# A later load of v, its scaling one chunk on, and three places in the order of the seven-product steps

## The chip, the cores and the metric

The kernel runs on one core of one Trainium2 chip. The core has five engines with queues of their own: TensorE (PE in the profile; PEld is its loading of weights), VectorE (DVE), ScalarE (ACT), GpSimd (POOL) and SyncE (SP, which here only issues transfers). The time is that of one execution on the device, in microseconds; less is better. The figure to compare is the median of the runs.

## The reference: what is computed

A recurrent attention with decay (4 batches, 8 heads, 768 positions, 64 numbers per head) feeds a two-layer network with 3072 tokens, 512 inputs and 2048 hidden units. All is in 32-bit floats, but the two weight matrices come as 64-bit floats and are turned into 32-bit ones by the kernel.

```python
for t in range(S):
    state = gamma[None, :, None, None] * state + np.einsum('bhd,bhe->bhde', k[:, :, t], v[:, :, t])
    y[:, :, t] = scale * np.einsum('bhd,bhde->bhe', q[:, :, t], state)
x = y.transpose(0, 2, 1, 3).reshape(B * S, H * D)
h = x @ w_in
g = h - np.tanh(h)
out = g @ w_out
```

## The kernel before

**Attention in chunks.** The 3072 tokens are cut into 24 chunks of 128 (`ci`), six for each batch. q and v are multiplied by powers of the decay (`scale`, line 267), and k and q are needed transposed. The first eight chunks are worked in a piece order written by hand (lines 991 to 1012). From chunk 8 on the transposing is done by a DMA: ACT copies k and q into a tile `apart` (`set_apart`, line 314), ACT issues a transfer that writes it to a scratch tensor `rows` in HBM, and SP issues a transposing DMA from `rows` into `kqT` (`turn_by_dma`, line 321), which has to wait until `rows` has landed. PE then makes the chunk's products (`products`, line 339: first k with v at L350, then the transposed k and q at L356) and its outputs (`outputs`, `outputs_rest`, L405), and ACT copies the outputs into `xT` (`keep_x`, L451).

**The network in tiles.** A tile (n, m2) is 256 tokens by 256 hidden units. An "up" product makes h in PSUM, ACT and DVE make g of it (th, u, q0, q1, large; `shrink_...`), and "down" products of g with w_out are summed in PSUM. For n of 0 to 3 the products are ordinary: eight matmuls at L471 for an up, eight at L560 for a down. From n = 4 (`FAST_UP`, `FAST`) both are done with seven products in place of eight: the up in two groups, U (products 1, 5, 7, 6) and V (2, 3, 4) at L801. Between them `up_take` (L806) copies what U left in PSUM out on ACT, POOL adds pairs of it (`up_pairs`, L811), V overwrites a part of the same PSUM bank, so it waits for the copy, and `up_add` (L816, L818) adds the pairs on DVE. The down products of these tiles are at L700.

**What sets the order.** Every engine works in the order in which the program issues to it. The loop from line 1100 on runs over steps `s`, one tile each; `with_chunk` puts a chunk step (`chunk_step`, line 1072) into two of every three steps: in steps 9, 11, 12, 14, 15, 17, 18 and so on to 35 and 37. The chunk step of `ci` makes the products of chunk ci + 2, loads k, q and v of chunk ci + 4 (`load_chunk`, all on SP), and turns chunk ci + 3. The step before it scales q and v of chunk ci + 3 on POOL (lines 1109 to 1111), in front of the weight conversions of that step. SP's queue thus reads, chunk by chunk: k, q, v, the transposing DMA, then weight loads. k and q have two buffers each, v has four.

Step 32 (`FIRST_UP`) is the first with seven products up. In steps 32 and 34 `downs(lag, half)` still issues down products of the old kind (L560) for the last tiles before, four matmuls for each half of a tile; step 33 has none, since the distance between up and down grows by one there. `middle()` (line 1066) gives ACT the square q0 and DVE the multiplication by it.

For n = 6 and 7 a list of pieces, `tile_order` (line 1256), orders each tile: U, the copy c, the pairs P, ..., M, V, R, E, the addition a, .... M and E issue as many of the open down products as `MIDDLE` and `END` say for that tile; M stops at the end of a run of eight tiles, and R then reads the sums out.

Of the kernel before, what the change touches and what calls it, by code (L numbers as in the profile page):

```python
# [31 lines left out]
def kernel(  # L32
# [25 lines left out]
    nc = tc.nc  # L58
# [64 lines left out]
    def weight_ends(i):  # L123


        f, r = divmod(i, 2 * NC)
        if r < NC:
            cols = ts(NC * f + r, P)
            rows = w_in[:, cols].rearrange("(k two p) n -> p two k n", two=2, p=P)

            return w1[:, :, cols], [
                (ds(0, P), 0, rows[:, 0]),
                (ds(0, D), 1, rows[D:, 1]),
                (ds(D, D), 1, rows[:D, 1]),
            ]
        m = NC * f + r - NC
        return w2[:, m], w_out[ts(m, P)]

    def load_weights(i):
        if i >= NW:  # L140
            return
        dst, src = weight_ends(i)
        raw = None
        if w_out.dtype != F32:
            if EARLY <= i < EARLY + 2 * len(rooms):
                raw = rooms[(i - EARLY) // 2][:, (i - EARLY) % 2]
            else:
                raw = stage.tile([P, 2 * BANK], U32, tag="raw", name=f"raw_{i}", bufs=3)
            raws[i] = raw
        if not isinstance(src, list):  # L150
            if raw is None:
                nc.sync.dma_start(out=dst, in_=src)
            else:
                nc.sync.dma_start(out=raw, in_=src.bitcast(U32))
            return
        if raw is not None:
            dst = raw.rearrange("p (c n) -> p c n", c=NC)
        for r, k, w in src:
            nc.sync.dma_start(out=dst[r, k::2], in_=w if raw is None else w.bitcast(U32))
# [87 lines left out]
    def load_one(ci, which, queue=nc.sync):  # L247
        if ci >= NCH:
            return
        b, j = divmod(ci, CPB)  # L250
        nm, src = ("k", "q", "v")[which], (k, q, v)[which]
        t = inp.tile([P, H, D], F32, tag=nm, name=f"{nm}_{ci}", bufs=4 if nm == "v" else 2)
        rows = src[b, :, ts(j, P), :]
        if nm == "q" and ci < WIDE:
            queue.dma_start(
                out=t.rearrange("p (i r) d -> p i (r d)", r=RUN),
                in_=rows.rearrange("(g i) (p r) d -> p g i (r d)", i=2, r=RUN),
            )
        else:
            queue.dma_start(out=t, in_=rows.rearrange("h p d -> p h d"))  # L260
        loaded.setdefault(ci, {})[which] = t

    def load_chunk(ci):
        for which in range(3):
            load_one(ci, which)

    def scale(ci, which, engine):
        if ci >= NCH:
            return
        t, g = loaded[ci][1 + which], (gw if ci < WIDE else gq, gv)[which]  # L270
        out_ = t
        if which == 0 and ci < WIDE:
            if not wide:
                room = mid.tile([P, 2, RUN, 2, D], F32, tag="apart", name="wide", bufs=1)
                wide.extend([room[:, i % 2] for i in range(WIDE)])
            out_ = loaded[ci][1] = wide.pop()
            out_ = out_.rearrange("p r i d -> p i r d")
            t, g = (x.rearrange("p (i r) d -> p i r d", r=RUN) for x in (
                t, g[:, ts(ci % CPB, H)][:, :, None].to_broadcast([P, H, D])))
        else:  # L280
            g = g[:, ts(ci % CPB, H)][:, :, None].to_broadcast([P, H, D])
        engine.tensor_tensor(out_, t, g, op=ALU.mult)  # L282
# [205 lines left out]
    def shrink_factor(n, m2):  # L488
        q0 = work("q0", 1)
        nc.scalar.activation(q0, shrinking[n, m2]["u"], AF.Square, bias=bias0)  # L490
        shrinking[n, m2]["q0"] = q0
# [194 lines left out]
    def fast_down(n, m2, first, last, half=None):  # L686
        some = fast_order(first)[{None: slice(7), 0: slice(4), 1: slice(4, 7)}[half]]
        if first and 1 in some:
            fast_banks(n)
        fast_products(n, m2, first, last, some)  # L690
# [40 lines left out]
    def fast_end(n):  # L731


        todo, store = sums_of(n)
        for x in ("p1", "c11", "v"):
            todo[x]()
        for x in ("w", "c22", "x", "c21", "c12"):
            def step(x=x):
                todo[x]()
                if x[:2] == "c1" or x == "c21":  # L740
                    store(int(x == "c21"))
            ending.append(step)
# [62 lines left out]
    def up_take(n, m2):  # L805
        nc.scalar.copy(out=odd_room[0], in_=hps[n, m2])  # L806
# [53 lines left out]
    def part(j, n, m2, first, last):  # L860
        down(n, m2, j, first, last)
        if last:
            add_up(n, m2, j)

    def downs(lag, half=None):

        while len(waiting) > lag:
            tile_ = waiting[0] if half == 0 else waiting.pop(0)
            if tile_[0] >= FAST:
                fast_down(*tile_, half=half)  # L870
                if tile_[3] and half != 0:
                    fast_end(tile_[0])
            else:
                for j in range(2) if half is None else (half,):
                    part(j, *tile_)
            if half is not None:
                return
# [145 lines left out]
    FIRST = 8  # L1023
# [3 lines left out]
    with_chunk = {h // 2: FIRST - 3 + i for i, h in enumerate(halves)}  # L1027
# [5 lines left out]
    FIRST_UP = steps.index((FAST_UP, 0, True, False))  # L1033
# [30 lines left out]
    before = None  # L1064

    def middle():

        if before and len(shrinking[before]) == 2:
            shrink_factor(*before)
            shrink_third(*before)  # L1070
# [29 lines left out]
    for s in range(BEGUN, steps.index((PAIRED - 2, 0, True, False))):  # L1100
        n, m2, first, last = steps[s]
        fast = n >= FAST_UP
        ci = with_chunk.get(s)

        falls_back = s == FALL or s in behind_up
        lag = LAG + int(s >= FALL)
        if ci is not None and not falls_back:
            chunk_step(ci)
        if s + 1 in with_chunk:
            for which in range(2):  # L1110
                scale(with_chunk[s + 1] + 3, which, nc.gpsimd)
        for i in with_weights.get(s, []):
            convert(i)
        if fast:
            fast_up(n, m2, (1, 5, 7, 6))
            up_take(n, m2)
        else:
            for i in range(2):
                up(n, m2, i)
        if falls_back and ci is not None:  # L1120
            chunk_step(ci)
        if before and ci is not None:
            turn_and_see(ci)
        if ci == NCH - 2:
            outputs(ci + 1)
            see(ci + 1)
        for i in with_weights.get(s, []):
            load_weights(i + 3)
        waiting.append(steps[s])
        if fast:  # L1130
            if before and ci is None:
                shrink_factors(*before)
                shrink_last_factor(*before)
            up_pairs()
            for make in with_sums.get(s, []):
                make()
            downs(lag, 0)
            if not before:
                downs(lag, 1)
            fast_up(n, m2, (2, 3, 4))  # L1140
            up_add(n, m2)
            shrink_begin(n, m2)
            if before:
                shrink_end(*before)
                if before[0] >= FAST:
                    fast_sums(*before)
            downs(lag, 1)
            end_some(1)
            shrink_two(n, m2)
            before = n, m2  # L1150
            if s + 1 not in with_chunk:
                middle()
        else:
            shrink_begin(n, m2)
            shrink_factors(n, m2)
            shrink_multiply(n, m2)
            downs(lag)
            shrink_last_factor(n, m2)
            shrink_end(n, m2)
            for make in with_sums.get(s, []):  # L1160
                make()
# [72 lines left out]
    def ripe():  # L1234
# [13 lines left out]
        "M": lambda n, m2, *_: next_products(MIDDLE[PAIRS * (n - PAIRED + 2) + m2]),  # L1248
        "E": lambda n, m2, *_: next_products(END[PAIRS * (n - PAIRED + 2) + m2]),
        "R": lambda *_: end_run(),  # L1250
# [4 lines left out]
    }  # L1255
    tile_order = """U c P q1- f2- x M V R E a S l- thA uA f3- f4- f0A q0A R f1A s"""
    MIDDLE = (2, 4, 4, 4, 6, 3, 4, 5, 4, 5, 5, 5, 4, 6, 5, 5)
    END = (0, 1, 2, 3, 4, 0, 2, 4, 2, 0, 1, 3, 1, 0, 2, 1)
    for n in range(PAIRED - 2, PAIRED):
        for m2 in range(PAIRS):  # L1260
            waiting.append((n, m2, m2 == 0, m2 == PAIRS - 1))
# [2 lines left out]
            before = n, m2  # L1264
# [4 lines left out]
    for j in range((NB - FIRST_BLOCK) * PAIRS):  # L1269
# [7 lines left out]
        before = other  # L1277
# [71 lines left out]
```

## Time and profile before

| | us |
|---|---|
| median of 3 runs | 693.65 (693.26 to 694.98) |
| the profiled execution, its own time | 695.14 |
| its span | 693.4 |

The granted clock of TensorE was 1.00 through the whole span. The span holds three stretches: the attention and ordinary products to about 285 us, the seven-product steps to about 478 us, and seven-product blocks of two tiles to the end. The slices of the page (40 of 17.3 us each, in tenths) show where transfers are heavy:

```profile
POOL 1632454555355586877854464364343446454271
PEclk9999999999999999999999999999999999999999
DMA  8892267968788566500000000000000000000000
```

Nearly all transfers are over by 295 us. Queue q1 is that of SP, q10 that of ACT; q8 and q14 carry instructions. The loads of k, q and v are 256 KB each in rows of 256 B, the write of `rows` is 512 KB:

```profile
## 3 DMA queue, kind: packets, MB, share of 16 engines
q1 hardware_dynamic: 116736, 50.08, 28.2%
q10 hardware_dynamic: 2736, 8.83, 3.6%
q8 instruction: 48, 0.79, 0.5%
...
rows<-apart ACTq DMA_DIRECT2D x16, 512.0 KB, 4.8
k<-in_k_dram SPq DMA_DIRECT2D x24, 256.0 KB, 4.8
q<-in_q_dram SPq DMA_DIRECT2D x24, 256.0 KB, 4.9
v<-in_v_dram SPq DMA_DIRECT2D x24, 256.0 KB, 5.9
```

The last column is the median time from issue to landing. In the timelines, a row gives the start, the length, the engine, the line, what is written and read, the shape and the number of instructions merged; in brackets stand the idle time of the engine before it and what ended that.

### The profile page before, as it was taken

To read this page: it belongs to the slowest core of one execution; us is meant where nothing else is said; L and a number is where in the kernel's file an instruction comes from. 1 tells how busy PE (TensorE), PEld (TensorE's weight loads), DVE (VectorE), ACT (ScalarE), POOL (GpSimd) and SP (SyncE) were. 2 spreads that over 40 slices of the span, in tenths; PEclk is the share of its full clock that TensorE was granted. 3 is DMA by queue.
4 is the path that set the end of the run, shared out by engine and by line. 5 is a ranking of instruction groups with operands and counts; after the bars stand their busy time and mean duration, and the time that the engine had idled before them with its cause. 6 is when DMAs were issued, how large, how long until landed. Compare 5 with 4: busy or idle time off the path is not lost.

```text
span 693.4 us, 15454 instructions
## 1 busy us (share of the span) xinstructions
PE 684.4 (99%) x6092; PEld 557.5 (80%) x6092; DVE 531.0 (77%) x879; ACT 429.4 (62%) x817; POOL 356.7 (51%) x492
## 2 busy tenths in 40 slices
PE   8999999999999999999999999999999999999998
PEld 5776666667667667779999999999888888888886
DVE  4999999989798865677776787687878779668641
ACT  3787577776776855465555666566766666566520
POOL 1632454555355586877854464364343446454271
PEclk9999999999999999999999999999999999999999
DMA  8892267968788566500000000000000000000000
GB/s 223 228 279 67 85 170 205 233 163 218 209 191 222 160 167 180 157 33 1 1 1 16 17 1 31 1 1 30 2 1 31 1 1 30 1 0 31 1 30 31
DMA packets 119544, 59.89 MB, mean 86 GB/s; under 512 B 101680, under 2 KB 112560, under 8 KB 119472
## 3 DMA queue, kind: packets, MB, share of 16 engines
q1 hardware_dynamic: 116736, 50.08, 28.2%
q10 hardware_dynamic: 2736, 8.83, 3.6%
q8 instruction: 48, 0.79, 0.5%
q14 instruction: 24, 0.20, 0.1%
HBM read 35.83 MB, written 14.68 MB: 73 GB/s over the span
## 4 chain that ended last, share of the span: by engine, by line
PE 88%; DMA 6%; ACT 3%; DVE 2%; SPq 1%; issue 0%; ACTq 0%; DVEq 0%
PE h L801 14%; PE o L560 13%; PE h L471 13%; PE fast_t L700 12%; PE y L700 8%; PE fast_o L840 7%; PE h L840 7%; PE fast_o L700 6%; PE y L405 3%; DMA kqT<-rows 3%; DMA rows<-apart 3%; PE last_h L700 1%; PE s L356 1%; PE s L350 1%; ACT apart L318 1%; PE kqTp L298 1%
## 5 line engine op out<-in xcount | busy, mean ns | idle before, releaser
L471 PE MATMUL h<-xT,w 128*128 128x256 f32 x512 | 117.7, 382 | 0.0
L560 PE MATMUL o<-w,g 128*128 128x512 f32 x256 | 116.3, 596 | 0.0
L471 PEld LDWEIGHTS h<-xT,w 128*128 128x128 f32 x512 | 95.9, 190 | 21.5 <-issue 9.1
L560 PEld LDWEIGHTS o<-w,g 128*128 128x128 f32 x256 | 47.6, 190 | 46.7 <-issue 44.0
L850 POOL TENSOR_TENSOR fast_head<-fast_head 128x512 f32<-128x512 f32 x16 | 20.5, 1278 | 87.2 <-ACT fast_head L846 87.2
L490 ACT ACTIVATE q<-u,tab 128x512 f32<-128x512 f32 x88 | 63.6, 723 | 1.4
L509 DVE TENSOR_TENSOR th<-h,th 128x512 f32<-128x512 f32 x72 | 49.1, 682 | 19.3 <-ACT th L482 17.2
L208 POOL TENSOR_TENSOR low<-low,power 128x512 f32<-128x512 f32 x26 | 34.5, 1326 | 52.6 <-DVE power L201 40.3
L1166 ACT ACTIVATE th<-h 128x512 f32<-128x512 f32 x32 | 19.1, 597 | 51.5 <-DVE h L818 30.3
L513 DVE SCALAR_TENSOR_TENSOR h<-q,h 128x512 f32<-128x512 f32 x72 | 49.8, 692 | 1.0 <-ACT q L490 1.0
L217 POOL TENSOR_TENSOR w<-low,head 128x512 f32<-128x512 f32 x28 | 36.9, 1317 | 13.5 <-DVE low L208 6.4
L282 POOL TENSOR_TENSOR q<-q,tab 128x512 f32<-128x512 f32 x16 | 18.0, 1125 | 46.6 <-DMA q<-in_q_dram 46.6
L801 PEld LDWEIGHTS h<-xT,w 128*128 128x128 f32 x256 | 37.4, 191 | 5.5 <-ACT fast_head L806 2.3
L811 POOL TENSOR_TENSOR fast_head<-fast_head 128x256 f32<-128x256 f32 x32 | 23.4, 731 | 35.5 <-ACT fast_head L806 35.5
L801 PE MATMUL h<-xT,w 128*128 128x128 f32 x256 | 39.8, 278 | 0.5 <-ACT fast_head L806 0.5
L552 DVE COPY_PREDICATED g<-large,th 128x512 f32<-128x512 int32 x39 | 35.8, 918 | 3.9
L816 DVE TENSOR_TENSOR h<-h,fast_head 128x256 f32<-128x256 f32 x32 | 13.8, 431 | 31.2 <-PE h L801 26.2
L650 POOL TENSOR_TENSOR s<-g 128x128 f32<-128x128 f32 x38 | 18.9, 497 | 36.5 <-DVE g L552 29.6
L522 DVE SCALAR_TENSOR_TENSOR g<-q,h 128x512 f32<-128x512 f32 x32 | 22.0, 687 | 17.3 <-ACT q L1174 9.8
L1174 ACT ACTIVATE q<-u,tab 128x512 f32<-128x512 f32 x49 | 35.2, 719 | 0.0
L1179 ACT ACTIVATE large<-u,tab 128x512 f32<-128x512 f32 x49 | 35.0, 715 | 0.0
L484 ACT ACTIVATE th<-h 128x512 f32<-128x512 f32 x16 | 9.6, 598 | 40.3 <-DVE h L818 40.3
(298 smaller groups left out, 1874.1 us busy)
## 6 DMA issues: line engine op xcount, KB each, us to landing
rows<-apart ACTq DMA_DIRECT2D x16, 512.0 KB, 4.8
k<-in_k_dram SPq DMA_DIRECT2D x24, 256.0 KB, 4.8
q<-in_q_dram SPq DMA_DIRECT2D x24, 256.0 KB, 4.9
v<-in_v_dram SPq DMA_DIRECT2D x24, 256.0 KB, 5.9
raw<-in_moe_w_out_dram SPq DMA_DIRECT2D x12, 512.0 KB, 4.3
out_dram<-sum SPq DMA_DIRECT2D x22, 256.0 KB, 2.2
raw<-in_moe_w_in_dram SPq DMA_DIRECT2D x14, 256.0 KB, 4.0
raw<-in_moe_w_in_dram SPq DMA_DIRECT2D x28, 128.0 KB, 4.1
```

The lines of the kernel that those rows point to most:

```text
L217: engine.tensor_tensor(dst, low, head, op=ALU.add)
L471: nc.tensor.matmul(hp, w1[:, c, ts(2 * m2 + i, P)], xT[n // 2][:, c, ts(n % 2, TH)], start=(begins and c == 0), stop=(c == NC - 1), skip_g ...
L490: nc.scalar.activation(q0, shrinking[n, m2]["u"], AF.Square, bias=bias0)
L509: nc.vector.tensor_tensor(th, hp, th, op=ALU.subtract)
L513: nc.vector.scalar_tensor_tensor(hp, in0=shrinking[n, m2]["q0"], scalar=C0, in1=hp, op0=ALU.add, op1=ALU.mult)
L552: nc.vector.copy_predicated(flat, large.bitcast(I32), th)
L560: nc.tensor.matmul(o_p[n, j], gT[n, m2][:, i, ts(j, P)], w2[:, 2 * m2 + i], start=(first and i == 0), stop=(last and i == 1))
L700: nc.tensor.matmul(accs[n][k], left[k - 1], right, start=first and k in (1, 6, 7, 4), stop=last, skip_group_check=True)
L801: nc.tensor.matmul(hps[n, m2][:, ts(PLACE[k], P)], s_of[m2][k - 1][:, c], x_of[n][k - 1][:, c], start=(k == 1 and c == 0), stop=(c == 1), ...
L840: nc.tensor.matmul(hps[2 * b + i, m2][:, ts(place, TH)], s_of[m2][k - 1][:, c], x_of["block", b][k - 1][:, c], start=(k in (1, 5) and c == 0),
L1174: nc.scalar.activation(q1, shrinking[n, m2]["u"], AF.Square, bias=bias1, scale=math.sqrt(A))
L1179: nc.scalar.activation(large, shrinking[n, m2]["u"], AF.Relu, bias=bias_m)
```

## The change

There are five edits. The load of v leaves `load_chunk` and comes at the end of the step's issues, behind the transposing DMA and the step's weight loads. v of a chunk is scaled one chunk step later than before, so in the step just before the one that uses it; POOL still does q first. In step 32 the second half of an old down product is issued behind V rather than in front of it. `middle()` for the tile of step 33 is called behind the `up_take` of step 34 rather than at the end of step 33. Two numbers of `END` are smaller by one.

```diff
     def load_chunk(ci):
-        for which in range(3):
+        for which in range(2):
             load_one(ci, which)
...
         if s + 1 in with_chunk:
-            for which in range(2):
-                scale(with_chunk[s + 1] + 3, which, nc.gpsimd)
+            scale(with_chunk[s + 1] + 3, 0, nc.gpsimd)
+            if with_chunk[s + 1] + 2 >= FIRST:
+                scale(with_chunk[s + 1] + 2, 1, nc.gpsimd)
...
             fast_up(n, m2, (1, 5, 7, 6))
             up_take(n, m2)
+            if s == FIRST_UP + 2:
+                middle()
...
         for i in with_weights.get(s, []):
             load_weights(i + 3)
+        if ci is not None:
+            load_one(ci + 4, 2)
         waiting.append(steps[s])
...
             downs(lag, 0)
-            if not before:
-                downs(lag, 1)
             fast_up(n, m2, (2, 3, 4))
             up_add(n, m2)
             shrink_begin(n, m2)
...
             before = n, m2
-            if s + 1 not in with_chunk:
+            if s + 1 not in with_chunk and s != FIRST_UP + 1:
                 middle()
...
-    END = (0, 1, 2, 3, 4, 0, 2, 4, 2, 0, 1, 3, 1, 0, 2, 1)
+    END = (0, 1, 1, 2, 4, 0, 2, 4, 2, 0, 1, 3, 1, 0, 2, 1)
```

## The prediction

> **What bounds the kernel now.** I read the busy row first, then the list of waits for PE alone, then the timelines around each wait.
>
> ```profile
> PE 684.4 (99%) x6092; PEld 557.5 (80%) x6092; DVE 531.0 (77%) x879; ACT 429.4 (62%) x817; POOL 356.7 (51%) x492
> ...
> PE s L356 <- DMA kqT<-rows: 1.6, 3, 0.9
> ...
> PE y L405 <- ACT xT L451: 0.6, 1, 0.6
> PE h L801 <- ACT fast_head L806: 0.5, 2, 0.3
> ```
>
> PE is busy 99% of the span. The change removes no matmul, so it can only win back time in which PE stands still. The three lower rows are all of PE's waits between 100 and 420 us (us in total, times, longest); after 420 us the list names none. What a wait costs is more than its gap:
>
> ```profile
> 168.14 1.03 PE L471 MATMUL h<-xT,w 128*128 128x256 f32 x4
> 169.10 0.46 PE L405 MATMUL y<-a,v 64*64 64x64 f32 x16
> 169.38 0.65 PE L350 MATMUL s<-v,k 64*64 64x64 f32 x32
> 170.62 0.69 PE L356 MATMUL s<-kqT 64*64 64x64 f32 x32 [0.59 <-DMA kqT<-rows]
> ```
>
> From the start of L350 to that of L356 takes 0.47 where nothing waits; here it takes 1.24, so a gap of 0.59 costs 0.77. The same reading gives 0.37 at 119 us, 0.77 at 170, 1.07 at 184, 0.19 at 197 (all kqT, sum 2.40); 0.73 at 296 (xT); 0.33 at 303 and 0.46 at 412 (up_take's copy). **All of it is 3.9 us, 0.56% of the time**: the ceiling of the gain.
>
> **Edit 1: v behind the transposing DMA.** The chain before kqT is: ACT copies k and q apart, ACT writes 512 KB of rows, SP waits for them and issues the transposing DMA, which lands 4.3 us later (its median). SP in that stretch:
>
> ```profile
> 159.00 4.05 SPq L260 DMA_DIRECT2D v<-in_v_dram  x1
> 166.21 2.11 SPq L330 DMA_TRANSPOSE kqT<-rows  x1
> 168.43 1.84 SPq L159 DMA_DIRECT2D raw<-in_moe_w_in_dram  x3
> 170.37 0.54 SPq L260 DMA_DIRECT2D k<-in_k_dram  x1
> 171.02 0.52 SPq L260 DMA_DIRECT2D q<-in_q_dram  x1
> 171.59 4.81 SPq L260 DMA_DIRECT2D v<-in_v_dram  x1
> 179.75 1.89 SPq L330 DMA_TRANSPOSE kqT<-rows  x1
> ```
>
> v is the last load before each transpose, and rows takes 6.6 and 7.5 us to land against a median of 4.8. The Trainium skill, page DMA: Bandwidth & Descriptors (section "Issuing engines are not separate DMA queues"), says that transfers from SP and ACT end up on the same 16 engines and interleave. By that rule v slows rows by up to its own time, 0.9 us (q lands at 179.51, v at 180.42); both transposes would come up to 0.9 earlier, and 0.77 + 0.9 would be won. The row says otherwise. These are all the packets of 179.2 to 180.2 us:
>
> ```profile
> DMA packets 63, 0.02 MB, mean 16 GB/s; under 512 B 63, under 2 KB 63, under 8 KB 63
> ## 3 DMA queue, kind: packets, MB, share of 16 engines
> q1 hardware_dynamic: 63, 0.02, 7.0%
> ```
>
> One engine, SP's queue alone, 63 packets: that is v's share on one engine (1024 rows of 256 B over 16), and it starts when the last of rows (q10) is through. The window 165.85 to 167.1 shows the same (68 packets, q1 alone). The late engine is the one that also fetched 16 KB of instructions (queue q8, one packet in each of these two stretches). So v, being last, delays rows hardly at all; its own load is what ends late, and nobody needs it then. I take 0.1 won at 170.
>
> Where v goes matters more. The order of the built program shows it behind the transpose and one weight load. Where two steps lie between chunk steps, SP has a pause there (141.1 to 144.9, say) and v is free. Where one step lies between, k and q follow at once: v then stands **ahead of k and q**. In the stretch 168 to 181 this puts up to 0.9 us more in front of q, and of rows on the late engine: kqT at 184 lands between 0.9 later and, if the missing tail helps after all, 0.9 earlier. I take 0, since the volume between the two transposes is the same. At 197 likewise 0: the DMA share is 0.97 from 181 to 192 and 1.02 from 192 to 200, and the same bytes precede the transpose.
>
> v itself has time: issued at about 169.7, scaled at 180.7; the slowest v of that stretch took 8.8 to land. Its slot (four buffers) was freed a step earlier. Its former load also blocked SP for 4 to 5 us, but the transpose behind it was waiting for rows anyway.
>
> **Edit 2: v scaled a chunk on.** POOL does q, then v, as before; the v is now the one that PE needs in the very next chunk step. POOL's wait for v (17.4 us in 11 times) goes, and is worth nothing: PE waits for POOL nowhere after 20 us. What is new is PE's L350 behind POOL's v, behind q's landing. In most steps v's scale ends 0.8 us or more ahead of L350 (181.7 against 182.5 is the tightest). One place is too late:
>
> ```profile
> 116.21 1.39 POOL L282 TENSOR_TENSOR q<-q,tab 128x512 f32<-128x512 f32 x1 [7.19 <-DMA q<-in_q_dram]
> ...
> 117.56 1.22 POOL L282 TENSOR_TENSOR v<-v,tab 128x512 f32<-128x512 f32 x1
> ...
> 118.56 0.69 PE L350 MATMUL s<-v,k 64*64 64x64 f32 x32
> ```
>
> L350 would start at about 118.85 instead of 118.56, with 0.2 of restart; L356 then finds kqT landed (119.40). One wait takes the other's place: cost 0.1. Behind POOL's q stand the two scales and the weight conversions, which PE needs a step later. Edits 1 and 2 together: **0.0**, between -1.9 (0.9 later at 184, 1.0 at 119) and +2.4.
>
> **Edit 3: half of the old down product behind V** (first seven-product step, before 292 us). PE does U, 4 matmuls of L560, V, 4 of L560, instead of 8 in a row: V 1.72 us earlier. h is then added to on DVE, read by ACT (th, u), and only then come up_take and the two xT copies for which PE waits at 296.74. But the addition also needs POOL's pairs, which end at 292.03 and get the last chunk's v scale (1.05) put in front: about 293.0, where DVE begins at 293.17 now. Gain 0.2; without the extra scale it would be the whole 0.56 and its restart; nothing at worst.
>
> **Edit 4: q0 behind up_take at 302.**
>
> ```profile
> 301.64 0.72 ACT L490 ACTIVATE q<-u,tab 128x512 f32<-128x512 f32 x1
> 302.26 0.57 ACT L806 COPY fast_head<-h 128x512 f32<-128x512 f32 x1
> ```
>
> U's last matmul began before 300.8; L806 stood behind L490 alone. Swapped, it ends near 302.2, before PE's L560 does (302.55). The 0.33 goes. DVE's third multiplication comes 0.6 later, but the one after it waits for q1 (ends at 303.45) in any case: cost 0 to 0.1 off the path.
>
> **Edit 5: END (2, 3) to (1, 2).**
>
> ```profile
> 411.35 0.60 PE L700 MATMUL fast_t<-w,s 128*128 128x256 f32 x2
> ...
> 411.60 0.59 ACT L806 COPY fast_head<-h 128x512 f32<-128x512 f32 x1 [0.37 <-PE h L801]
> ...
> 412.24 0.71 PE L801 MATMUL h<-xT,w 128*128 128x128 f32 x4 [0.30 <-ACT fast_head L806]
> ```
>
> Between U and V of the fifth tile only one product (two matmuls, 0.43) was left in the run, too few for the copy. With one product fewer after each of two earlier tiles, three are left: 1.29 us. U starts 0.86 earlier, L806 about 0.8 earlier, V follows without a wait. The 0.46 goes; the sum of products is equal from there on.
>
> **Sum:** 0.1 - 0.1 + 0.2 + 0.33 + 0.46 = 1.0 us. Against its own execution: 695.14 (span 693.4 and 1.8 around it) becomes 694.1. The median of the runs shown is 1.5 lower, 693.65, and becomes **692.6**.
>
> **Rivals.**
> - *All kqT waits go* (2.4 of the 2.4, or most): the late engine of the new run is another, or rows lands sooner without v's load. For it: rows needs 4.3 us where it is quick, and 2 us sooner is all that is asked. Against it: the packets above. With edits 3 to 5: 3.4 to 3.9, **690.2**. Chance 0.38.
> - *v ahead of q*: q lands up to 0.9 later where one step lies between chunks; POOL scales q, then v, and L350 waits, and kqT follows. It decides once q lands after 180.4 (179.51 now). Price 1.0 at 119 and 0.9 at 184, less the 1.0 of the other edits: slower than before, **694.5**. Chance 0.12.
> - *Edits 3 to 5 only move their waits* (ACT's or DVE's next instruction is late instead), v does nothing: 693.6. Chance 0.05.
> - My forecast: 0.45, by itself 691.7 to 693.4.
>
> A difference of 0.3% (2.1 us) is about what a measurement tells from none. Faster by more: the first rival mostly (0.33) and the lower end of mine (0.05); slower by more: the second where edits 3 to 5 win nothing either (1.9, to 695.6) and something is added (0.06). The range 689.9 to 694.4 leaves out the ends of both.
>
> **What would show it.** PE's waits on L806 gone at 303 and 412; the one on xT at 296 shorter; a wait of L350 on POOL's v near 119; rows as slow as now near 160 and 173 with v gone from behind q; kqT's wait at 184 still there. If the list of PE's waits has no kqT left, the first rival is right. It is wrong if instructions are fetched at other moments, since the late engine then changes.

## The result, and the profile after

| | before | after |
|---|---|---|
| median, us | 693.67 (20 runs, 692.70 to 694.98) | 692.18 (20 runs, 691.26 to 694.63) |
| ratio, 95% interval | | 0.9978 (0.9969 to 0.9987) |
| profiled execution: own time, span | 695.14, 693.4 | 691.43, 689.6 |

The change wins 1.5 us, 0.22%: real, since the interval ends below 1, and inside the 0.3% within which the prediction called it "the same". The two profiled spans differ by 3.8 us, two and a half times the gain; where the rest comes from is one of the questions below.

From the page of the changed kernel, the busy row (engine, busy time and share, instructions) and three rows of its transfers (the last column is the median time from issue to landing):

```profile
PE 682.7 (99%) x6092; PEld 556.9 (81%) x6092; DVE 525.1 (76%) x879; ACT 429.3 (62%) x817; POOL 357.2 (52%) x492
...
rows<-apart ACTq DMA_DIRECT2D x16, 512.0 KB, 4.4
...
q<-in_q_dram SPq DMA_DIRECT2D x24, 256.0 KB, 4.8
v<-in_v_dram SPq DMA_DIRECT2D x24, 256.0 KB, 4.8
```

PE has the same number of instructions and is as full as before. v lands in 4.8 where it took 5.9, rows in 4.4 where it took 4.8, q in 4.8 where it took 4.9. The list of PE's waits between 100 us and the end, which held kqT, xT and L806 before, is empty. By the prediction's own test ("if the list of PE's waits has no kqT left, the first rival is right") the rival has it. That test had to be put to a second execution of each kernel.

### The profile page after: what moved, and what is told of

Same layout as the page of the kernel before. It is cut to its first block, busy times and chain, and to the rows that moved or that the text cites. A ratio compares the mean times of both kernels' runs of the same rounds, so it can differ in the third digit from the quotient of the medians.

```text
span 689.6 us, 15450 instructions
## 1 busy us (share of the span) xinstructions
PE 682.7 (99%) x6092; PEld 556.9 (81%) x6092; DVE 525.1 (76%) x879; ACT 429.3 (62%) x817; POOL 357.2 (52%) x492
## 4 chain that ended last, share of the span: by engine, by line
PE 96%; DMA 1%; SPq 1%; ACT 0%; DVE 0%; issue 0%; ACTq 0%
PE o L560 16%; PE h L471 16%; PE h L801 15%; PE fast_t L700 12%; PE y L700 9%; PE fast_o L840 7%; PE h L840 7%; PE fast_o L700 6%; PE y L405 4%; PE last_h L700 2%; PE s L350 1%; PE s L356 1%; DMA k<-in_k_dram 1%; PE kqTp L298 1%; DMA q<-in_q_dram 1%; SPq L260 0%
## 5 line engine op out<-in xcount | busy, mean ns | idle before, releaser
L1169 ACT ACTIVATE th<-h 128x512 f32<-128x512 f32 x32 | 19.1, 598 | 51.7 <-DVE h L818 30.4
L801 PEld LDWEIGHTS h<-xT,w 128*128 128x128 f32 x256 | 37.5, 191 | 5.3 <-issue 1.2
L801 PE MATMUL h<-xT,w 128*128 128x128 f32 x256 | 39.7, 278 | 0.0
L816 DVE TENSOR_TENSOR h<-h,fast_head 128x256 f32<-128x256 f32 x32 | 13.8, 431 | 28.9 <-PE h L801 19.0
L522 DVE SCALAR_TENSOR_TENSOR g<-q,h 128x512 f32<-128x512 f32 x32 | 22.0, 688 | 17.0 <-ACT q L1177 9.1
L451 ACT COPY xT<-y 128x256 f32<-128x256 f32 x48 | 15.6, 379 | 29.6 <-PE y L405 29.5
```

The lines of the kernel that those rows point to most:

```text
L801: nc.tensor.matmul(hps[n, m2][:, ts(PLACE[k], P)], s_of[m2][k - 1][:, c], x_of[n][k - 1][:, c], start=(k == 1 and c == 0), stop=(c == 1), ...
```

## The experiments

The cost of a wait is taken much as in the prediction, from start to start of the instructions on either side, less the median of such a pair, in the one profiled execution of each kernel; the slow restart behind the wait is counted in, so that before has 2.48 for the prediction's 2.40. Costs under 0.15 are left out. "462" is a pause that no list of before has; the column xT keeps a remainder of 0.16 where the trace names no wait at all.

| kernel | median (runs) | before beside it | ratio, 95% interval | kqT | L350 on v | xT, 296 | L806, 302 | L806, 411 | 462 |
|---|---|---|---|---|---|---|---|---|---|
| before | 693.67 (20) | | | 2.48 | | 0.77 | 0.34 | 0.46 | |
| before_again | 692.92 (1) | | | | | 0.37 | 0.34 | 0.46 | |
| after | 692.18 (20) | 693.67 | 0.9978 (0.9969, 0.9987) | | | 0.16 | | | 0.20 |
| after_again | 692.76 (1) | | | 0.87 | | 0.16 | | | 0.20 |
| after_5 | 692.90 (12) | 693.99 | 0.9985 (0.9969, 1.0002) | 0.27 | | 0.16 | | | 0.19 |
| order_only | 693.83 (12) | 694.41 | 0.9990 (0.9974, 1.0006) | | | 0.16 | | | 0.20 |
| order_5 | 693.24 (12) | 693.99 | 0.9986 (0.9972, 1.0001) | 0.50 | | 0.16 | | | 0.20 |
| no_end | 692.83 (12) | 693.99 | 0.9982 (0.9966, 0.9998) | 0.37 | | 0.16 | | 0.46 | |
| v_only | 693.83 (12) | 694.41 | 0.9990 (0.9973, 1.0007) | 0.23 | | 0.65 | 0.34 | 0.46 | |
| v_5 | 693.62 (12) | 693.99 | 0.9994 (0.9979, 1.0009) | 2.02 | 0.35 | 0.57 | 0.34 | 0.46 | |
| scale_late_only | 694.34 (12) | 693.66 | 1.0016 (1.0001, 1.0031) | 1.12 | 0.36 | 0.23 | 0.34 | 0.46 | |
| v_ahead | 693.82 (12) | 693.66 | 1.0007 (0.9995, 1.0020) | | | 0.23 | 0.54 | 0.46 | |
| no_v | 693.88 (12) | 693.66 | 1.0003 (0.9989, 1.0016) | 0.36 | | 0.20 | 0.34 | 0.46 | |
| v_twice | 706.81 (5) | 693.66 | 1.0180 (1.0157, 1.0203) | 7.92 | | 0.26 | 0.34 | 0.46 | |

The three columns from 302 on are steps: each cost has one value (but for v_ahead's 0.54) and goes and comes with one edit. The column kqT has any value, within one and the same program. The column xT is neither; the section on edit 3 below says what it follows.

### The same programs once more

No edit; one profiled execution of each.

> The kernel before, unchanged, for a second profile. Its first profiled execution took 695.1 us, 1.5 above the median of 20. If the kqT waits of 2.4 us are the same in every execution: 2.3 to 2.5 us of them here too. If they come and go with the moments at which instructions are fetched: less, around 1 us, in an execution near the median; the waits at 296, 303 and 412 (1.5 us) the same to 0.1 us in both cases.

> The changed kernel, unchanged, for a second profile. Its first profiled execution took 691.4 us, 0.8 below its median. If v's place frees kqT for good: again no wait of PE between 100 and 690 us. If it only makes the wait rarer: some kqT wait of 0.2 to 1 us in an execution at or over the median of 692.2.

The list of PE's waits of before_again, from 100 us to the end (who waits on what: us in total, times, longest):

```profile
PE h L801 <- ACT fast_head L806: 0.5, 2, 0.3
PE y L405 <- ACT xT L451: 0.2, 1, 0.2
```

No kqT in it, with v where it always was; and after_again has one of 0.7 (0.87 with its restart) with v moved. From the issue of rows to that of the transposing DMA, mean of the first nine turns, the first profile took 5.80, before_again 4.77; the changed kernel took 4.62, 4.71 and 4.73 in its three profiles. **The 2.4 us of kqT in the profile before were a feature of that one execution**, not of the order of the loads. The prediction laid late rows to the DMA engine that also fetched instructions. The trace does not say which engine a packet ran on. In the first profile two of the 16 KB instruction fetches took 2.69 and 3.04, about 160 and 173 us, beside two of the rows that came late; in after the longest of this stretch took 1.99. But rows is as late beside ordinary fetches: 6.93 and 6.57 in v_5 and 6.20 in after_again, where no fetch beside it took over 1.17. So long fetches are not needed for it, and the cause **stays open**.

### Each half of the change

order_only and order_5 are before with edits 3 to 5, v_only and v_5 before with edits 1 and 2; the parts of the diff are those shown above.

> Edits 3, 4 and 5 (the three places in the order) without 1 and 2 (v as before). My theory: these edits bring 1.0 of the 1.5 us measured, so the ratio to before is 0.9985 (0.9976 to 0.9994); the waits of PE on L806 at 303 and 412 us are gone, the one on xT at 296 is gone or short, and the waits on kqT near 119, 170 and 184 are there as before. Rival (v's move brings nearly all): ratio 1.000.

> Edits 1 and 2 (v loaded behind the transposing DMA, scaled a chunk on) without 3 to 5. My theory as predicted: v's own part is 0, ratio 1.000, with kqT still waited for at 170 or 184. Rival (the profile of after, where no kqT wait is left): 1.0 to 2.4 us faster, ratio 0.9986 to 0.9965, and no wait of PE on kqT; the three waits at 296, 303 and 412 stay.

> Edits 3 to 5 alone. Theory: 0.9985 to 0.999 of before, that is 0.8 to 1.2 us, the same as after_5. Rival: 0.999 to 1.0, with after_5 lower by 0.001 or more.

> Edits 1 and 2 alone. Theory: 0.9995 to 1.0005 of before. Rival: 0.9985 to 0.9995, since waits for kqT become rarer.

> The changed kernel once more, beside the next three on the same chip. Theory (v's place is worth next to nothing, the three places in the order carry the gain): 0.9985 to 0.999 of before, within 0.0007 of order_5. Rival (the two v edits carry a part of it): 0.998 and at least 0.001 below order_5.

Side by side (order_5, v_5, after_5) the medians were below that of before by: edits 3 to 5 0.75, edits 1 and 2 0.37, all five 1.09. The parts add up (1.12), and the larger one is the order. But the intervals are 1.0 us to either side, so that none of the three, nor the difference between after_5 and order_5 (0.34), can be told from zero; order_only and v_only had 0.58 each. The medians alone do not show which half wins; the stretch of the seven-product steps, under "The sum" below, does. after_5 and order_5 came out as the theory had them, 0.0001 apart, though the intervals are fifteen times as wide; v_5 at 0.9994 fell a hair to the rival's side.

### v's scale late, v's load where it was

```diff
-            for which in range(2):
-                scale(with_chunk[s + 1] + 3, which, nc.gpsimd)
+            scale(with_chunk[s + 1] + 3, 0, nc.gpsimd)
+            if with_chunk[s + 1] + 2 >= FIRST:
+                scale(with_chunk[s + 1] + 2, 1, nc.gpsimd)
```

> Edit 2 alone: v loaded in its old place, scaled a chunk on. My theory: POOL's wait for v (17.4 us in the first profile of before) goes and PE gains nothing by it, ratio 1.000 (0.999 to 1.001); near 119 us PE's L350 waits for POOL's v up to 0.5 us where q lands late. Rival (the gain of edits 1 and 2 comes from POOL being ahead): ratio 0.999 or less, with the wait on xT at 296 gone.

The predicted wait of L350 on POOL's v at 119 us is there, 0.36, with a kqT wait of 1.12 behind it. It is there again in v_5, whose list of waits has

```profile
PE s L350 <- POOL v L282: 0.2, 1, 0.2
```

and in neither v_only nor any profile of the full change. POOL's v stands behind q's landing there: q landed at 117.05 in scale_late_only and at 116.06 in v_5, at 114.15 in after. So this wait too depends on how soon a transfer lands, and the late scale alone makes the kernel, if anything, slower (1.0016; the interval just clears 1, one of eleven in the table, so it is no more than a hint).

### Where v's load stands, and what it weighs

v_ahead loads v in front of k and q, with the late scale:

```diff
     def load_chunk(ci):
-        for which in range(3):
+        for which in (2, 0, 1):
             load_one(ci, which)
```

no_v leaves out v's loads from chunk 9 on, so its output is not the reference's; a chunk gets an older one's v, already scaled (four tiles, kept from the last loads). POOL still multiplies it, by q's table in place of v's:

```diff
     def load_one(ci, which):
+        if which == 2 and ci > 8:
+            loaded.setdefault(ci, {})[2] = kept[ci % 4]
+            return
...
+        if which == 2:
+            kept[ci % 4] = t
...
-        t, g = loaded[ci][1 + which], (gw if ci < WIDE else gq, gv)[which]
+        t, g = loaded[ci][1 + which], (gw if ci < WIDE else gq, gv if ci <= 8 else gq)[which]
```

v_twice adds, behind v, a copy of v's chunk to a scratch place in HBM, so 256 KB read and 256 KB written:

```diff
     def load_chunk(ci):
         for which in range(3):
             load_one(ci, which)
+        if ci < NCH:
+            b, j = divmod(ci, CPB)
+            again = dram.tile([H, P, D], F32, tag="again", name=f"again_{ci}")
+            nc.sync.dma_start(out=again, in_=v[b, :, ts(j, P), :])
```

> v loaded first of the three (v, k, q, then the transposing DMA) and scaled a chunk on. My theory: the bytes in front of the transpose are the same, but q lands up to 0.9 us later than in before (4.8 us from issue in its second profile, so 5.3 to 5.7), rows 0 to 0.9 later, and L350 or L356 wait in some chunks: ratio 1.000 to 1.003. Rival (order within the group makes no difference): ratio and waits as in before, 1.000.

> The kernel before, leaving out the loads of v from chunk 9 on (the four v tiles there are used again, multiplied by another table, so the output is not the reference's); POOL's scaling stays. This is the ceiling of what v's load can cost where it stands. My theory (v, last in its group, costs the transposes next to nothing): the write of rows in the first nine turns takes 4.5 to 4.8 us, as in the second profile of before (4.77), and the ratio is 0.9985 to 1.000. Rival (v in front of the transpose slows it, and the changed kernel wins by taking it away): rows 4.0 us or less, no kqT wait, ratio 0.997 or less.

> The kernel before with one more transfer of v's 256 KB (into a scratch tensor in HBM, read by nobody) on SP's queue right behind v, so in front of each transposing DMA. My theory (what stands behind q on SP's queue is not in the way of rows): rows at most 0.3 us later, 5.0 in the first nine turns, ratio 1.000 to 1.002. Rival: each 256 KB behind q costs rows 0.5 to 0.9 us, kqT waits at 119, 170, 182 and others, ratio 1.003 to 1.008.

With no v at all rows took 4.38 to the issue of the transposing DMA (first nine turns, one profile). With v in its old place it took 4.71 to 5.80 in five profiles, in its new place 4.62 to 5.11 in six: v costs rows some 0.3, if the lowest is taken, what the move gives back of that is lost in the spread, and the time without v does not change (1.0003). v in front of k and q delays q as it should (issue to landing 5.88 in the mean from 93 us on, 4.76 to 5.39 in the other profiles but v_twice, whose landings cannot be matched), and the time does not change either (1.0007). There is slack for that much.

v_twice is far slower than both expectations had it, but not by what they argued about. Its lines of code are numbered 4 higher: L360 is L356 of before. First PE's waits, then the wait of SP's queue before the longest of them, then SP there (start, length):

```profile
PE s L360 <- DMA kqT<-rows: 7.3, 3, 4.0
```

```profile
SPq L260 <- DMA rows<-apart: 5.0, 1, 5.0
```

```profile
114.06 0.37 SPq L260 DMA_DIRECT2D k<-in_k_dram  x1
114.53 0.53 SPq L260 DMA_DIRECT2D q<-in_q_dram  x1
115.11 0.84 SPq L260 DMA_DIRECT2D v<-in_v_dram  x1
116.00 0.72 SPq L269 DMA_DIRECT2D again<-in_v_dram  x1
116.77 4.10 SPq L334 DMA_TRANSPOSE kqT<-rows  x1
```

rows was not late here: issued at 109.78, it had landed by 114.00, 4.2 later (6.8 in before). What was late is SP. It stood 5.0 us in front of **k's** load until rows had landed, and then issued k, q, v and the copy, all four, before the transposing DMA: that went out 2.8 after rows had landed. In after k was issued at 107.57, long before, and the transposing DMA at 113.45, 0.02 behind the landing. It also took longer, with those four transfers just ahead of it: PE's L360 was let go at 124.57, 7.8 behind the issue, where in after the DMA landed after 4.9. In the trace k's load and rows report their landing on one semaphore here, and in after on two: the extra transfer has shifted which transfers share one. The same holds at the third of PE's waits, where k was held till 197.0 and the transposing DMA went out 2.9 behind rows' landing; at the second it was the copy that shared the semaphore and was held, and the DMA went out 0.8 behind. No other profile has SP wait for rows in front of anything but the transposing DMA.

So v_twice does not tell what 256 KB more in front of the transpose cost by their bytes. The copy is no second v either: it moves as 8 packets of 32 KB, which take 1.39 us each, where v's rows are packets of 256 B. A copy whose semaphore is not that of rows was not run. Three waits that cost 7.9 together are not all that was lost, either: 13 in the medians, 10.5 in the profiled execution (704.13 against the median 693.66). The rest is in the last section.

### Edit 5 taken out

```diff
-    END = (0, 1, 1, 2, 4, 0, 2, 4, 2, 0, 1, 3, 1, 0, 2, 1)
+    END = (0, 1, 2, 3, 4, 0, 2, 4, 2, 0, 1, 3, 1, 0, 2, 1)
```

> The changed kernel with END as it was. Theory: the wait on L806 in the tile at 410 us is back (0.46 in all), and the pause of 0.27 at 462 us is gone with it, since the lighter runs of down products are what brings U so close behind V there: in all 0.1 to 0.2 us slower than after_5, 1.000 beside it. Rival: the pause at 462 stays (edits 3 and 4 cause it, by moving the tiles against the transfers and copies): then edit 5 is worth its whole 0.46, and this kernel is that much slower.

The wait is back, as one row of its list of PE's waits:

```profile
PE h L801 <- ACT fast_head L806: 0.3, 1, 0.3
```

and the pause at 462 us is gone. Two rows of after's timeline there, and then one of no_end's:

```profile
461.06 0.36 ACT L723 COPY fast<-fast_t 128x256 f32<-128x256 f32 x1
...
461.45 0.69 DVE L522 SCALAR_TENSOR_TENSOR g<-q,h 128x512 f32<-128x512 f32 x1 [0.45 <-ACT fast L723]
```

```profile
462.27 0.69 DVE L522 SCALAR_TENSOR_TENSOR g<-q,h 128x512 f32<-128x512 f32 x1 [0.19 <-ACT q L1177]
```

With edit 5 DVE's multiplication starts only when ACT has also ended the copy behind the square that it reads, 0.26 later, and PE's next U stands until 0.15 after it has ended. All five profiles with edit 5 have this, none of the nine without. Counted up to the first block of two tiles, edit 5 brings 0.45 at 411 us and gives 0.27 back: 0.18. In the medians after_5 and no_end are 0.07 apart the other way, which is nothing. The expectation held in place and size, but not for its reason: DVE's and ACT's instructions around 462 us, and the semaphores that they wait on, are alike in both traces; the counts that are waited for are not kept in them, so why L522 goes by the later of two instructions in one kernel **stays open**.

## Why the prediction was right, and where it was not

692.6 was foretold and 692.18 measured. Step by step:

**v's place worth nothing (edit 1): right.** That v, being last, hardly holds up rows was read from 63 packets of one engine; no_v puts it at some 0.3 us of rows and at no time that can be measured (the interval reaches 0.8 us to the faster side), where the rule of the interleaving transfers, as the prediction worked it out, allowed up to 0.9. The packets of before at 178.5 to 179.0, where by their spacing one engine is left, show interleaving and why it is cheap: between two packets of rows (4096 B, 159 ns each) stands one of SP's queue (256 B, 18 ns). rows has 144 packets, 9 on an engine, so one such packet ahead of each makes 0.16 (an estimate from these). "Ahead of k and q" was a danger by the queue's order, and v_ahead shows that the loads bear it.

**"kqT's wait at 184 still there": wrong.** The step took four waits of one execution for the kernel's own, and carried 2.4 us of them over into the time after. Three other profiles with v loaded and scaled as before (before_again, order_only, order_5) show 0, 0 and 0.5. The median of before was 1.5 below the profiled execution's time, and it was mostly these waits that put that execution above it: its span is 2.3 longer than before_again's, which is 2.5 of kqT and 0.4 of xT, less a start-up that was 0.6 quicker. The prediction subtracted the 1.5 as an offset and so took most of these waits out again without knowing it. The ceiling of "3.9 us", and the 0.38 put on the rival, came from an unlucky execution.

**"L350 on POOL's v at 119, 0.1": right as a mechanism, mis-sized.** It costs 0.35 where it occurs, in two of seven profiles with the late scale and v not in front.

**Edit 3, "0.2, since POOL's pairs get the last v scale in front": another reason than the one given, and a size that is right only in the mean.** Rows of POOL and DVE in after:

```profile
286.55 1.04 POOL L282 TENSOR_TENSOR v<-v,tab 128x512 f32<-128x512 f32 x1
287.55 0.72 POOL L811 TENSOR_TENSOR fast_head<-fast_head 128x256 f32<-128x256 f32 x1
...
288.96 0.43 DVE L816 TENSOR_TENSOR h<-h,fast_head 128x256 f32<-128x256 f32 x1 [2.94 <-POOL fast_v L640]
```

and the same in no_end:

```profile
288.87 1.04 POOL L282 TENSOR_TENSOR v<-v,tab 128x512 f32<-128x512 f32 x1
289.87 0.72 POOL L811 TENSOR_TENSOR fast_head<-fast_head 128x256 f32<-128x256 f32 x1
...
290.62 0.43 DVE L816 TENSOR_TENSOR h<-h,fast_head 128x256 f32<-128x256 f32 x1 [3.76 <-POOL fast_head L811]
```

In after the pairs end at 288.27, and the addition starts 0.7 later, 0.1 behind the end of V's last matmul (288.85; the bracket names a POOL instruction that ended meanwhile). Counted from the start of the second group of U's matmuls, DVE's L816 starts at 6.38 in each of the eight profiles without edit 3 and at 4.67, V's 1.71 earlier, in five of the six with it. Only in no_end (5.68) are the pairs last, as the prediction had it. It goes with the moment at which the last q lands, since POOL's work stands behind it. Among the profiles with the late scale, q lands 9.4 to 9.8 ahead of that matmul in five, and the pairs end at 4.0 to 4.5; in no_end it is 8.1 and 5.65, in v_only and v_ahead 7.8 and 7.7, and 5.93 and 6.23. In the profile that the prediction was made from it was 7.7, and the prediction's pairs (1.05 behind their old end, 6.29) were right for that. With q earlier there was room for v's scale. Even the 0.7 that no_end wins at L816 ended the xT wait.

How large that wait is without edit 3 was not seen by the prediction either. Over the remainder of 0.16 it is 0.61 in before, 0.49 in v_only, 0.41 in v_5, 0.21 in before_again and 0.04 to 0.10 in the other four, though L816 starts at 6.38 in all eight. It follows the end of DVE's next instruction, L818 (7.69, 7.57, 7.49, 7.29, and 7.15 to 7.18). DVE and POOL in before, then in scale_late_only:

```profile
293.59 0.73 POOL L640 TENSOR_TENSOR fast_v<-w 128x256 f32<-128x256 f32 x1
293.63 0.84 DVE L818 TENSOR_TENSOR h<-fast_head 128x128 f32<-128x128 f32 x1
```

```profile
293.43 0.30 DVE L818 TENSOR_TENSOR h<-fast_head 128x128 f32<-128x128 f32 x1
293.43 0.88 POOL L640 TENSOR_TENSOR fast_apart<-fast_v,w 128x256 f32<-128x256 f32 x1
```

The same addition takes 0.30 or 0.84. In each of the fourteen profiles this L818 ends 0.30 after its start or, where a POOL instruction that began before it is still running, 0.15 or 0.16 after that one's end, whichever is later; in scale_late_only it is POOL that takes longer, 0.88 for its 0.73. So 0.54 of the 0.61 in the prediction's own profile came of where POOL's work happened to fall, and edit 3, with V early, is clear of it. In that profile the term was a third of what there was to win; over the eight profiles the mean is 0.25. That the 0.2 comes so near is luck, since the pairs that it was worked out from were not in the way.

**Edit 4, 0.33: right.** L806 at 302 us waits 0.34 in seven and 0.54 in one of the eight profiles without it, and in none of the six with it.

**Edit 5, 0.46: right where it was looked at, and 0.27 too high,** since the pause at 462 us was not foreseen. "The sum of products is equal from there on" was no proof that nothing else would move.

**The sum, 1.0.** The stretch from the first seven-product up to the first block of two tiles (from PE's first L801 to its first L840) has no start-up in it, and no kqT wait in any profile. It takes 190.46 to 190.48 in the five profiles with edits 3 to 5, 190.66 in no_end, and 191.17 to 191.73 in the eight without them, v's edits or not: edits 3 to 5 win 0.7 to 1.25 there, 0.9 in the mean. This shows what the medians could not, that the order carries a gain. That the sum fits so well is in part luck, its terms were less right: edit 5 gave less than its 0.46, edit 3 more than its 0.2 in the prediction's own profile. The medians' gain was 1.1 for after_5, within that range, and 1.5 in the first comparison, above it; what that has in excess no edit was shown to give, and start-up and kqT differ by more between executions.

**The rivals.** "All kqT waits go" had its sign in the first trace and lost it in the second. "v ahead of q" had its late q in v_ahead, and no wait and no change of time came of it there (1.0007); its L350 behind POOL's v came in two other profiles, at 0.35 for the 1.0 that it feared. "Edits 3 to 5 only move their waits" was partly right, of edit 5.

## What to carry to other kernels

Before waits of a tenth of a per cent are summed from a profile, take a second profile of the same kernel: a wait that comes back to the hundredth (0.46 at 411, 0.34 at 302) belongs to the order of the program and can be removed, and one on a transfer that comes and goes (0 to 2.5 us) belongs to the execution. An edit that moves a few matmuls to cure one place should be followed to the end of the run of tiles, since the next tile with the same tight spot may pay. Where an added transfer costs more than its bytes can explain, ask what its queue waited for: in v_twice that was k's load, held until rows had landed, and everything behind it came late. And the length of an instruction on DVE is no constant where POOL works beside it (0.30 or 0.84 for one and the same addition): ask which of the two began first.

## What was not expected of the hardware

**After a standstill of 4 us TensorE's clock stood at half.** v_twice by stretches around its longest wait (stretch, length, busy time of PE, PEld, DVE, ACT and POOL with instruction counts, granted clock, DMA share, GB/s):

```profile
121.00:123.50 2.50, 0.00 (x0) 0.00 (x0) 0.00 (x0) 0.00 (x0) 2.28 (x3) 1.00 1.18 358
123.50:130.30 6.80, 5.73 (x84) 3.73 (x85) 3.02 (x6) 3.22 (x9) 4.13 (x4) 0.50 1.12 244
```

PE's last matmul before the wait ended near 120.6. 2.9 us into the standstill the clock fell from 1.00 to 0.50 and stayed there for 6.8 us, 5.7 of them after PE was at work again. The matmuls of L564 took up to twice as long; what PE lost between the two chunk steps is 6.9 us (19.5 from one to the next against 12.6), where the wait with its restart explains 4.2. The other two waits, 1.4 and 1.9 long, left the clock at 1.00. Both expectations for v_twice had priced a wait at its own length; the waits alone (7.9) were beyond them, and the clock made 2.7 of the 6.9 that the longest one lost. The page TensorE: Matmul & The Clock Gate of the Trainium skill (Part 1, on the clock gate) gives half clock after an idle window of some 3.4 us; here it fell 2.9 after the last matmul. Of the 12.7 us by which its span is longer than after's, the waits and the half clock make 10.6, the start-up 1.5, and the rest, 0.6, is about what edits 3 to 5 win.

**The start-up is not the same twice.** At the first down product, about 47 us, two profiles of one program differ by 2.05 us (after and after_5), and all fourteen by up to 2.6; the difference is carried to the end. It is larger than the whole gain, and with kqT it is the reason that single spans say nothing about a change of this size.
